# The order of a fused attention and MoE kernel: first loads on SyncE, one early sine, and a new table of offsets

## The chip, the core and the metric

One NeuronCore of a Trainium2 chip. The metric is the device time of one execution in microseconds. TensorE is called PE here, VectorE DVE, ScalarE ACT, GpSimd POOL and SyncE SP.

## What is computed

```python
kv  = einsum('bhsd,bhse->bhde', k, v)             # batch 8, heads 8, sequence 576, head size 64
out = einsum('bhsd,bhde->bhse', q, kv)
out = out / sqrt(mean(out * out, -1) + 1e-6) * g_norm
x   = out.transpose(0, 2, 1, 3).reshape(4608, 512)
h   = x @ w_in                                     # w_in is 512 x 2048
y   = (h * cos(h)) @ w_out                         # w_out is 2048 x 512, y is 4608 x 512
```

All inputs are fp32, w_in and w_out arrive as float64.

## The kernel before

A product of fp32 accuracy is made of three fp32r matmuls, from a high and a low part of each factor (xhi and xlo, ghi and glo; a weight tile wi or wo holds both of its parts). So every weight and every activation passes a "split": a cast on ACT for the high part, a difference on DVE for the low one. For a weight, which arrives in 512 KB tiles, there are some three wide DVE operations and two on ACT (`w_part`, L1034).

The 4608 tokens are nine chunks of 512. The first three go through 48 steps, 16 for each chunk: stage 1 multiplies one 128-column block j of w_in with the four pairs of heads p of x (four groups of three matmuls into a bank, `stage1_part`, L1111), ACT and DVE make h*cos(h) and its split (`act_part`), and stage 2 adds the product with block j of w_out to four accumulators acc0 to acc3, one for each 128 tokens (`stage2_part`, L1179). The other six chunks are taken in three twos by a scheme of seven products (`quad_part`, L1483), whose combined weights are written to DRAM as wq and read back as wi and wo tiles, and a gather with weights out of wod. When an accumulator is full, ACT copies it to one of five slot tiles, and a DMA stores it to out (`out_part`, L1212).

The attention of chunks 0 and 1 is the front. For each pair of heads, k, v and q are loaded, kv is made of 64x64 matmuls (`kv_front_part`), q is transposed through PE, x is made and summed, DVE and POOL make 1/rms (rinv), PE turns the scaled x, and ACT and DVE split it into xhi and xlo with g as a scale (`x_front_part`, L796, `x_norm`, L976). g lies twice in gcol (`g_part`, L552), once for each head of a pair. These early tiles borrow the buffers of weights, so k, v and q appear in the rows as wi and wo tiles. Matmuls on zeros keep PE at work while it would wait.

The order of every engine's instructions is set before the program is built, by a planner (`class Order`, L52). Each part is a generator that asks for time on an engine with a priority; the planner keeps a clock for each engine and starts what can begin first, and of those the one with the lowest priority number. Priorities come from due times of the steps (`due`, L320) plus an offset from a table, `haste` (L327), read by `put_off` (L461) and `gate`. An engine name with a star (DVE*) takes a port that DVE and POOL share; with two engines named, the planner picks. The chip then runs each engine's list in that order, with semaphores for the data.

Nearly all loads and stores are issued by SP through `dmas` (L520), eight in flight at a time; the ninth waits until the first has landed. In `first_loads` (L590) ACT issues k and v of the first pair of heads, the warming sine, and g. All instructions are recorded at L239, since a helper emits them, so rows are told apart by their tiles.

Of the kernel before, what the change touches and what calls it, by code (L numbers as in the profile page):

```python
# [16 lines left out]
AF = mybir.ActivationFunctionType  # L17
# [168 lines left out]
def tile_kernel(  # L186
# [91 lines left out]
    pool.memset(warm, 0.0)  # L278

# [40 lines left out]
    def due(i):  # L320
# [7 lines left out]
        ('acc', 0): 48.4, ('acc', 1): 9.5, ('acc', 10): 311.8, ('acc', 12): -210.7, ('acc', 13): -56.2,  # L328
        ('acc', 14): -112.1, ('acc', 15): 26.9, ('acc', 16): -26.6, ('acc', 17): 2190.7, ('acc', 18): 147.3,
        ('acc', 19): -18.0, ('acc', 2): 101.2, ('acc', 20): 0.5, ('acc', 21): 402.0, ('acc', 24): 404.7,  # L330
        ('acc', 25): 109.7, ('acc', 26): -287.8, ('acc', 27): 8.4, ('acc', 28): 182.6, ('acc', 29): -175.7,
        ('acc', 30): 7.6, ('acc', 31): -58.8, ('acc', 32): 47.5, ('acc', 33): 317.1, ('acc', 34): 1784.0,
        ('acc', 35): 708.7, ('acc', 36): 47.8, ('acc', 37): 20.4, ('acc', 38): 18.1, ('acc', 39): 1.9,
        ('acc', 4): 57.7, ('acc', 40): 636.6, ('acc', 41): -56.3, ('acc', 42): 142.5, ('acc', 43): -345.9,
        ('acc', 44): 240.0, ('acc', 45): 0.1, ('acc', 46): -281.1, ('acc', 47): -52.1, ('acc', 5): 10.5,
        ('acc', 6): 602.4, ('acc', 7): 113.2, ('acc', 8): -14.3, ('acc', 9): 20.2, ('act', 0): 0.5,
        ('act', 1): -263.8, ('act', 10): -60.6, ('act', 11): -55.6, ('act', 12): 14.3, ('act', 13): -237.4,
        ('act', 14): -452.5, ('act', 15): 594.3, ('act', 16): -153.5, ('act', 17): -140.9, ('act', 18): -873.0,
        ('act', 19): -297.3, ('act', 2): 9.0, ('act', 20): 37.2, ('act', 21): -211.4, ('act', 22): 73.3,
# [8 lines left out]
        ('gate keep in', 11): -163.6, ('gate keep in', 12): -211.4, ('gate keep in', 13): -79.1,
        ('gate keep in', 14): -1472.4, ('gate keep in', 15): -26.1, ('gate keep in', 2): 3.7,
        ('gate keep in', 3): -524.9, ('gate keep in', 4): 66.0, ('gate keep in', 5): -51.5,  # L350
        ('gate keep in', 6): -142.9, ('gate keep in', 7): -8.0, ('gate keep in', 8): 108.0,
# [1393 lines left out]
```

## Time and profile before

| | us |
|---|---|
| median of 3 runs | 843.07 (843.03 to 843.53) |
| the profiled execution, its own time | 844.05 |
| its span in the trace | 842.2 |
| PE busy in the span | 825.9 |
| DVE busy | 613.8 |
| ACT busy | 498.2 |
| POOL busy | 227.6 |
| first stage-1 product starts | 35.02 |

Busy time of PE is time in which a matmul is under way. The span is what the trace covers; the execution's own time has some 1.85 us around it. Matmuls overlap, so the distance between starts tells what one costs, and a count of matmuls times that distance tells how much work a stretch of PE rows holds.

### The profile page before, as it was taken

The page shows a single profiled execution, that of the slowest core. Times are in us where ns is not written, and L with a number is a line of the kernel's source. Part 1 is how long each engine was busy: PE and PEld are TensorE (multiplying, and loading weights), DVE is VectorE, ACT ScalarE, POOL GpSimd, SP SyncE. Part 2 cuts the span into 40 slices and gives each one's busy share as a digit, 9 for nine tenths or more (in the row PEclk, how much of TensorE's full clock was granted, in tenths as well). Part 3 has the DMA queues.
Part 4 walks back from the last instruction along what each step waited for, and adds up shares of the span by engine and source line. Part 5 has one row for each costly group of instructions (what it writes and reads, how often), then busy time and mean ns, then how long its engine had stood idle before and what let it go on. Part 6 is the DMA issues. An engine that isn't in the chain of part 4 may idle for free.

```text
span 842.2 us, 12749 instructions
## 1 busy us (share of the span) xinstructions
PE 825.9 (98%) x4424; PEld 681.1 (81%) x4424; DVE 613.8 (73%) x963; ACT 498.2 (59%) x974; POOL 227.6 (27%) x150
## 2 busy tenths in 40 slices
PE   8799999999999999999999999999999999999998
PEld 7678888888888887888887888888788888888886
DVE  3999994469598878669999968878899575444221
ACT  4879983445265565557786657767675464444321
POOL 3310034724427762010324620122438000000000
PEclk9999999999999999999999999999999999999999
DMA  9997535665765577598898767777557566763664
GB/s 301 299 399 275 176 113 190 194 176 155 236 184 189 152 205 269 175 335 254 267 278 233 216 190 183 211 248 201 176 200 240 175 195 191 229 215 105 223 206 145
DMA packets 150399, 181.20 MB, mean 215 GB/s; under 512 B 73920, under 2 KB 113600, under 8 KB 150336
## 3 DMA queue, kind: packets, MB, share of 16 engines
q1 hardware_dynamic: 149824, 179.68, 69.0%
q8 instruction: 35, 0.57, 0.3%
q10 hardware_dynamic: 512, 0.72, 0.2%
q14 instruction: 28, 0.23, 0.1%
HBM read 143.66 MB, written 36.70 MB: 214 GB/s over the span
## 4 chain that ended last, share of the span: by engine, by line
PE 81%; DMA 8%; DVE 5%; ACT 3%; issue 1%; SPq 1%; POOL 0%; DVEq 0%; ACTq 0%; POOLq 0%
PE bank L239 42%; PE acc L239 40%; DMA wi<-in_q_dram 2%; DVE r L239 1%; DMA wo<-wq 1%; DMA x<-slot 1%; DMA out_dram<-slot 1%; DMA wi<-in_v_dram 1%; DVE slot L239 1%; ACT slot L239 1%; DMA sg<-in_v_dram 1%; DMA slot<-part 1%; SPq L239 1%; DVE glo L239 1%; DMA wq<-slot 1%
## 5 line engine op out<-in xcount | busy, mean ns | idle before, releaser
L239 PE MATMUL acc<-wo,ghi 128*128 128x512 f32 x1152 | 355.7, 390 | 1.3 <-ACT slot L239 1.3
L239 PEld LDWEIGHTS acc<-wo,ghi 128*128 128x128 f32 x1152 | 215.4, 188 | 46.3 <-ACT slot L239 2.2
L239 PE MATMUL bank<-wi,wo 128*128 128x512 f32 (+2 forms) x1092 | 244.2, 380 | 4.2 <-DMA wo<-wq 2.0
L239 PEld LDWEIGHTS bank<-wi,wo 128*128 128x128 f32 (+2 forms) x1092 | 191.8, 185 | 46.8 <-DVE glo L239 2.4
L239 PE MATMUL acc<-wo,glo 128*128 128x512 f32 x576 | 224.3, 389 | 0.0
L239 POOL TENSOR_TENSOR rinv<-ms,mhalf 128x16 f32<-128x16 f32 (+1 forms) x36 | 97.2, 2703 | 228.9 <-DVE ms L239 228.5
L239 PEld LDWEIGHTS acc<-wo,glo 128*128 128x128 f32 x576 | 108.1, 188 | 23.0
L239 PE MATMUL bank<-xhi,wi 128*128 128x512 f32 x320 | 99.8, 393 | 0.2 <-DVE slot L239 0.2
L239 DVE TENSOR_TENSOR wi<-bank,wi 128x512 f32<-128x512 f32 x72 | 49.5, 687 | 44.4 <-PE bank L239 35.9
L239 DVE TENSOR_TENSOR glo<-wo,ghi 128x512 fp32r<-128x512 f32 x58 | 42.5, 732 | 46.1 <-ACT ghi L239 45.8
L239 ACT ACTIVATE ki<-wi 128x512 int32<-128x512 f32 x72 | 45.1, 627 | 42.4 <-DVE wi L239 33.7
L239 PEld LDWEIGHTS bank<-xhi,wi 128*128 128x128 f32 x320 | 58.8, 188 | 13.5 <-DVE r L239 0.8
L239 ACT CAST ghi<-wo 128x512 fp32r<-128x512 f32 x61 | 37.8, 619 | 48.4 <-PE acc L239 47.8
L239 ACT ACTIVATE ki<-bank 128x512 int32<-128x512 f32 x72 | 42.6, 591 | 34.2 <-PE bank L239 29.4
L239 PE MATMUL bank<-xlo,wi 128*128 128x512 f32 x160 | 62.4, 390 | 0.0
L239 ACT COPY wi<-bank 128x512 f32<-128x512 f32 x72 | 41.9, 583 | 24.2 <-PE bank L239 23.6
L239 ACT ACTIVATE wo<-wo 128x512 f32<-128x512 f32 x61 | 38.4, 630 | 26.1 <-DVE wo L239 25.8
L239 DVE TENSOR_TENSOR glo<-r,ghi 128x512 fp32r<-128x512 f32 x60 | 44.0, 733 | 13.1 <-ACT ghi L239 10.6
L239 ACT ACTIVATE r<-r 128x512 f32<-128x512 f32 x60 | 37.8, 630 | 20.1 <-DVE r L239 19.6
L239 DVE SCALAR_TENSOR_TENSOR r<-bank,ki 128x512 f32<-128x512 f32 x51 | 34.8, 683 | 19.9 <-ACT ki L239 19.4
L239 ACT CAST ghi<-r 128x512 fp32r<-128x512 f32 x60 | 37.1, 618 | 17.4 <-PE acc L239 16.0
L239 DVE TENSOR_TENSOR r<-r,bank 128x512 f32<-128x512 f32 x51 | 34.5, 678 | 8.5 <-ACT r L239 8.4
(175 smaller groups left out, 1071.6 us busy)
## 6 DMA issues: line engine op xcount, KB each, us to landing
wo<-wod SPq DMA_DIRECT2D x96, 512.0 KB, 3.4
wo<-wq SPq DMA_DIRECT2D x84, 512.0 KB, 4.0
out_dram<-slot SPq DMA_DIRECT2D x35, 256.0 KB, 3.4
wo<-in_moe_w_out_dram SPq DMA_DIRECT2D x16, 512.0 KB, 9.6
wi<-in_moe_w_in_dram SPq DMA_DIRECT2D x16, 512.0 KB, 9.9
wod<-wo SPq DMA_DIRECT2D x16, 512.0 KB, 4.1
wq<-wi SPq DMA_DIRECT2D x24, 256.0 KB, 3.5
m<-in_k_dram SPq DMA_DIRECT2D x24, 256.0 KB, 4.4
```

The source lines that it names most:

```text
L239: return lambda *a, **kw: tc.keep_in_program_order(f(*a, **kw))
```

## The change

The warming sine stands right behind the memset of its tile, ahead of everything on ACT. The loads of k and v of the first pair, and of g, go through `dmas` on SP with priorities that put them early. g's doubling (`g_part`) waits for g's load alone, no longer for kv of the second pair of heads, and fires an event for which the split of every front x waits. The planner is told that the sum ms and the low part of a weight take the shared port of DVE, and that rinv takes 3.15 us of POOL instead of 3.0. Every number of `haste` is new.

```diff
     pool.memset(warm, 0.0)
+    act.activation(out=warm, in_=warm, func=AF.Sin)
...
     haste = {
-        ('acc', 0): 48.4, ('acc', 1): 9.5, ('acc', 10): 311.8, ('acc', 12): -210.7, ('acc', 13): -56.2,
+        ('acc', 0): 253.3, ('acc', 1): 234.7, ('acc', 11): -183.7, ('acc', 12): -84.3, ('acc', 13): -234.2,
...
     def g_part():
         yield "wait", [g_in]
-        yield "wait", [kv_in[0, 1]]
-        yield "run", [("ACT", 0.4)], -11.0
+        _, end = yield "run", [("ACT", 0.4)], -11.0
         for r in (slice(D, 2 * D), slice(0, D)):
             act.activation(out=gcol[r, :], in_=gcol[0:D, :], func=AF.Copy, scale=INV_2PI)
+        sched.fire(g_turns, end)
...
     def first_loads():
         kv_tiles[0, 0] = [wpool.tile([P, SF, D], F32, name=f"{kind}{j}") for kind, j in first_tags]
-        yield "run", [("ACT", 0.5)], -1e3
-        for t, src in zip(kv_tiles[0, 0], (k, v)):
-            act.dma_start(out=t, in_=src[0, 0:2].rearrange("h (p i) d -> (h p) i d", i=SF))
-        act.activation(out=warm, in_=warm, func=AF.Sin)
-        act.dma_start(out=gcol[0:D, :], in_=g_norm.rearrange("(d o) -> d o", o=1))
-        for ev, us in ((kv_in[0, 0], 1.9), (g_in, 0.1)):
-            _, end = yield "run", [("DMA", us)], -1e3
-            sched.fire(ev, end + DMA_LAT)
+        end = yield from dmas([
+            copies(t, src[0, 0:2].rearrange("h (p i) d -> (h p) i d", i=SF), 0.95)
+            for t, src in zip(kv_tiles[0, 0], (k, v))], -1e3)
+        sched.fire(kv_in[0, 0], end)
+
+    def g_load():
+        end = yield from dmas([copies(gcol[0:D, :], g_norm.rearrange("(d o) -> d o", o=1), 0.1)], -950.0)
+        sched.fire(g_in, end)
...
         slot = yield "take", tokens, prio
+        yield "wait", [g_turns]
         yield "run", [("ACT", act_us() + 0.08)], prio
...
-        yield "run", [("DVE", 0.17)], prio
+        yield "run", [("DVE*", 0.17)], prio
         ms = small.tile([P, TB], F32, name="ms")
...
-        yield "run", [("POOL", 3.0)], prio
+        yield "run", [("POOL", 3.15)], prio
...
-            e, end = yield "run", [("ACT", 0.57, 0.3), ("DVE", 0.36, 0.0)], prio
+            e, end = yield "run", [("ACT", 0.57, 0.3), ("DVE*", 0.36, 0.0)], prio
...
             if c == 0 and p == 0:
+                sched.spawn(g_load())
                 sched.spawn(g_part())
```

PE has the same matmuls after the change as before, 1152 + 576 of stage 2 and the rest alike; DVE has 14 instructions fewer, POOL 8 more, ACT 3 more (with three DMA issues fewer among them), SP three more.

SP from its first row on, before. ACT's first two rows before are the loads of k into wi_162 and of v into wo_163, the pair that kv0, the first kv product, needs.

```order
L239 DMA wi_164<-in_q_dram 128x2x256 x2
L239 DMA wo_167<-in_k_dram 128x576
L239 DMA wo_165<-in_k_dram 128x576
L239 DMA wi_169<-in_q_dram 128x2x256
L239 DMA wi_172<-in_k_dram 96x2x384
L239 DMA wi_170<-in_k_dram 128x576
L239 DMA wi_169<-in_q_dram 128x2x256
L239 DMA wi_168<-in_v_dram 128x576
L239 DMA wo_166<-in_v_dram 128x576
L239 DMA wi_174<-in_q_dram 96x4x128
L239 DMA wo_173<-in_v_dram 96x2x384
```

SP from its first row on, after the change. k of that pair goes into wi_163, v into wo_164.

```order
L239 DMA wi_163<-in_k_dram 128x576
L239 DMA gcol<-in_g_norm_dram 64x1
L239 DMA wi_170<-in_q_dram 128x2x256
L239 DMA wo_168<-in_k_dram 128x576
L239 DMA wi_171<-in_k_dram 128x576
L239 DMA wi_165<-in_q_dram 128x2x256
L239 DMA wo_166<-in_k_dram 128x576
L239 DMA wi_165<-in_q_dram 128x2x256
L239 DMA wo_164<-in_v_dram 128x576
L239 DMA wo_189<-in_moe_w_out_dram 128x512
L239 DMA wi_169<-in_v_dram 128x576
L239 DMA wo_172<-in_v_dram 128x576
```

k stands first and g second. v stands ninth, behind loads of k and q for the other pairs, and so behind the eight that may be in flight; a first w_out tile (wo_189) follows it.

PE's first rows behind the matmuls on zeros, before. A row of 64x64 is a kv product, one of ident and a wi tile a transpose of q, one of wo and m an x, one of ident and r a turn of the scaled x.

```order
L239 MATMUL bank0_204<-wo4_163,wi6_162 64x64 x18
L239 MATMUL bank1_227<-ident_125,wi7_164 128x128 x4
L239 MATMUL bank3_239<-ident_125,wi7_164 128x128 x4
L239 MATMUL acc2_247<-wo15_158,m0_237 128x2x64 x4
L239 MATMUL bank2_253<-ident_125,wi9_169 128x128 x4
L239 MATMUL bank0_270<-ident_125,wi9_169 128x128 x4
L239 MATMUL bank1_278<-wi8_168,wo7_167 64x64 x18
L239 MATMUL acc2_247<-ident_125,r0_299 128x128 x4
L239 MATMUL bank3_316<-wo6_166,wo5_165 64x64 x18
```

The same place after the change:

```order
L239 MATMUL bank0_204<-ident_126,wi9_170 128x128 x4
L239 MATMUL bank1_216<-ident_126,wi7_165 128x128 x4
L239 MATMUL bank2_225<-ident_126,wi7_165 128x128 x4
L239 MATMUL bank3_233<-wo4_164,wi6_163 64x64 x18
L239 MATMUL acc2_263<-wo15_159,m1_221 128x2x64 x4
L239 MATMUL bank0_270<-wi8_169,wo7_168 64x64 x18
L239 MATMUL bank1_299<-wo8_172,wi10_171 64x64 x18
L239 MATMUL acc0_328<-wo15_159,m0_211 128x2x64 x4
L239 MATMUL bank2_347<-ident_126,wi9_170 128x128 x4
L239 MATMUL bank3_357<-wo6_167,wo5_166 64x64 x18
L239 MATMUL acc1_385<-wo15_159,m1_353 128x2x64 x4
L239 MATMUL acc2_263<-ident_126,r0_381 128x128 x4
```

Three transposes of q come ahead of kv0, and no matmuls on zeros stand between them. All four kv products and all four x of chunk 0 come in one go; before, products of chunk 1 and zeros come between the third x and the fourth.

PE at the end of the chunk whose acc3 is the last to fill, and the start of the next chunk's accumulators, before:

```order
L239 MATMUL acc3_3940<-wo14_5121,ghi0_5159 128x512 x2
L239 MATMUL acc3_3940<-wo14_5121,glo0_5160 128x512
L239 MATMUL acc0_5270<-wo12_5149,ghi1_5202 128x512 x2
L239 MATMUL acc0_5270<-wo12_5149,glo1_5203 128x512
L239 MATMUL acc1_5280<-wo12_5149,ghi1_5202 128x512 x2
L239 MATMUL acc1_5280<-wo12_5149,glo1_5203 128x512
L239 MATMUL acc2_5287<-wo12_5149,ghi1_5202 128x512 x2
L239 MATMUL acc2_5287<-wo12_5149,glo1_5203 128x512
L239 MATMUL acc3_5295<-wo12_5149,ghi1_5202 128x512 x2
L239 MATMUL acc3_5295<-wo12_5149,glo1_5203 128x512
```

The same place after the change:

```order
L239 MATMUL acc3_4240<-wo15_5106,ghi0_5160 128x512 x2
L239 MATMUL acc3_4240<-wo15_5106,glo0_5161 128x512
L239 MATMUL acc0_5265<-wo12_5150,ghi1_5199 128x512 x2
L239 MATMUL acc0_5265<-wo12_5150,glo1_5200 128x512
L239 MATMUL acc1_5281<-wo12_5150,ghi1_5199 128x512 x2
L239 MATMUL acc1_5281<-wo12_5150,glo1_5200 128x512
L239 MATMUL acc2_5290<-wo12_5150,ghi1_5199 128x512 x2
L239 MATMUL acc2_5290<-wo12_5150,glo1_5200 128x512
L239 MATMUL bank1_5067<-wi0_4825,wo9_4846 128x512 x3
L239 MATMUL bank1_5067<-wi1_4837,wo9_4846 128x512 x3
L239 MATMUL acc3_5316<-wo12_5150,ghi1_5199 128x512 x2
L239 MATMUL acc3_5316<-wo12_5150,glo1_5200 128x512
```

Between acc2 and acc3 of the new chunk stands a pair of products of the seven-product scheme.

## Rows read from the trace of the kernel before

**Rows 1.** The page of the kernel before: its head, and part 1 (busy time of each engine, share of the span, instructions).
```profile
span 842.2 us, 12749 instructions
...
PE 825.9 (98%) x4424; PEld 681.1 (81%) x4424; DVE 613.8 (73%) x963; ACT 498.2 (59%) x974; POOL 227.6 (27%) x150
```
**Rows 2.** Busy time by stretch. Columns: the stretch, its length, then PE, PEld, DVE, ACT and POOL busy in us (with instructions), TensorE's granted clock, the busy share of the DMA engines, GB/s moved.
```profile
0.00:10.00 10.00, 7.87 (x94) 7.24 (x95) 1.48 (x4) 3.17 (x7) 4.38 (x13) 1.00 0.79 249
10.00:20.00 10.00, 8.01 (x150) 6.90 (x151) 6.01 (x14) 5.93 (x17) 2.59 (x2) 1.00 1.08 354
20.00:30.00 10.00, 7.98 (x130) 7.07 (x124) 9.24 (x20) 7.88 (x15) 3.94 (x3) 1.00 1.10 279
30.00:40.00 10.00, 7.79 (x98) 6.02 (x94) 9.37 (x19) 7.42 (x19) 3.72 (x2) 1.00 1.08 328
40.00:60.00 20.00, 19.98 (x125) 15.34 (x126) 19.83 (x36) 16.32 (x33) 3.62 (x2) 1.00 1.06 385
280.00:340.00 60.00, 58.03 (x255) 47.61 (x254) 45.60 (x69) 34.09 (x70) 29.38 (x23) 0.97 0.66 203
460.00:600.00 140.00, 138.81 (x682) 114.20 (x681) 117.79 (x180) 91.91 (x185) 40.94 (x19) 1.00 0.70 208
```
**Rows 3.** What PE waited for over the whole span. After the colon: us in total, times, the longest in us.
```profile
PE bank L239 <- DMA wo<-wq: 2.0, 1, 2.0
...
PE bank L239 <- DMA wo<-in_q_dram: 1.6, 1, 1.6
...
PE acc L239 <- ACT slot L239: 1.3, 2, 1.2
```
**Rows 4.** The timeline of the first 17 us, all engines. Columns: start us, length us, engine, line, operation, out<-in, shapes, count, and in brackets the idle time before with what ended it (ACTq and SPq are the issuing sides).
```profile
0.72 0.45 ACTq L239 DMA_DIRECT2D wi<-in_k_dram  x1
...
0.73 0.95 SPq L239 DMA_DIRECT2D wi<-in_q_dram  x2
...
1.73 1.28 ACT L239 ACT_TABLE_LOAD   x1 [1.73 <-issue]
...
6.08 1.26 PE L239 MATMUL bank<-wo,wi 64*64 64x64 f32 x36 [0.85 <-DMA wo<-in_v_dram]
...
8.61 1.16 PE L239 MATMUL acc<-wo,m 128*128 128x128 f32 x8 [0.24 <-ACT m L239]
...
9.82 0.42 PEld L239 LDWEIGHTS bank<-ident,wi 128*128 128x128 f32 x4 [0.25 <-DMA wi<-in_q_dram]
...
12.03 0.66 PE L239 MATMUL bank<-ident,wi 128*128 128x128 f32 x4 [1.55 <-DMA wi<-in_q_dram]
...
12.82 1.26 PE L239 MATMUL bank<-wi,wo 64*64 64x64 f32 x36
...
13.33 0.43 ACT L239 ACTIVATE gcol<-gcol 64x1 f32<-64x1 f32 x2
...
14.57 0.47 DVE L239 COPY wo<-bank 64x64 f32<-64x64 f32 x2 [0.72 <-ACT wo L239]
...
14.76 0.69 ACT L239 ACTIVATE xhi<-acc,gcol 128x512 fp32r<-128x512 f32 x1 [0.22 <-ACT wo L239]
15.47 0.75 DVE L239 SCALAR_TENSOR_TENSOR xlo<-acc,gcol,xhi 128x512 fp32r<-128x512 f32 x1 [0.44 <-ACT xhi L239]
```
**Rows 5.** DMA issues of the first 30 us: out<-in, issuing engine, operation, count, KB of each, median us from issue to landing.
```profile
wo<-in_v_dram SPq DMA_DIRECT2D x4, 288.0 KB, 7.4
...
wi<-in_v_dram SPq DMA_DIRECT2D x2, 288.0 KB, 9.1
wi<-in_k_dram ACTq DMA_DIRECT2D x1, 288.0 KB, 3.5
wo<-in_v_dram ACTq DMA_DIRECT2D x1, 288.0 KB, 4.7
```
**Rows 6.** The timeline of 33 to 41 us, first DVE, then PE (columns as in rows 4).
```profile
33.48 0.69 DVE L239 TENSOR_TENSOR wi<-sg,wi 128x512 fp32r<-128x512 f32 x1
34.09 0.68 DVE L239 SCALAR_TENSOR_TENSOR sg<-sg,m 128x512 int32<-128x512 int32 x1
...
35.02 0.70 PE L239 MATMUL bank<-xhi,wi 128*128 128x512 f32 x2
...
36.48 0.60 PE L239 MATMUL bank<-ident,wo 128*128 128x128 f32 x4
...
38.15 1.29 PE L239 MATMUL bank<-wo,m 128*32 128x128 f32 x20
40.02 0.66 PE L239 MATMUL bank<-ident,r 128*128 128x128 f32 x4 [0.58 <-DVE r L239]
```
**Rows 7.** Three views of the weight loads out of wq: their issues over the whole span on the page (columns as in rows 5), the chain of work that ended last at 327 us (start us, us, what), and PE's timeline from 325 us.
```profile
wo<-wq SPq DMA_DIRECT2D x84, 512.0 KB, 4.0
...
327.14 8.25 DMA wo<-wq
...
325.24 8.32 PE L239 MATMUL bank<-wi,wo 128*128 128x512 f32 x36
335.53 4.58 PE L239 MATMUL bank<-wi,wo 128*128 128x512 f32 x12 [1.97 <-DMA wo<-wq]
```
**Rows 8.** The chain of work that ended last, 458 to 464 us: start us, us, what.
```profile
458.28 3.88 DMA out_dram<-slot
...
462.27 0.61 ACT slot L239
```

More of the change, by code (lines that the diff above doesn't have):

```diff
@@ L348, in tile_kernel @@
[L348 to L351, printed above, removed]
-        ('gate keep in', 9): 48.8, ('gate keep out', 0): -620.3, ('gate keep out', 1): -60.3,
-        ('gate keep out', 10): -282.8, ('gate keep out', 11): 40.5, ('gate keep out', 12): 155.5,
@@ L360, in tile_kernel @@
-        ('gate load', 6): -2.1, ('gate load', 7): -35.3, ('gate sums', 0): 4.7, ('gate sums', 1): 1.5,
-        ('gate sums', 2): 63.8, ('gate sums', 3): -21.8, ('gate sums', 4): 45.9, ('gate sums', 5): -46.0,
-        ('gate sums', 6): 45.0, ('gate sums', 7): -43.4, ('gate x', 2, 0): -224.7, ('gate x', 2, 1): -89.5,
[17 rows of a table removed]
-        ('keep in', 7): -61.8, ('keep in', 8): 27.5, ('keep in', 9): 111.4, ('keep out', 0): 11.4,
-        ('keep out', 1): 126.8, ('keep out', 10): -168.2, ('keep out', 11): -60.7, ('keep out', 12): 62.6,
@@ new lines, in tile_kernel @@
+        ('gate keep out', 3): 1.0, ('gate keep out', 4): -4.7, ('gate keep out', 5): -126.4,
+        ('gate keep out', 6): 201.5, ('gate keep out', 7): -70.7, ('gate keep out', 8): -2.7,
+        ('gate keep out', 9): -12.4, ('gate kv', 4): -0.2, ('gate kv', 5): 5.6, ('gate kv', 7): 39.9,
+        ('gate load', 2): 5.7, ('gate load', 3): -24.0, ('gate load', 4): -99.1, ('gate load', 5): 63.5,
+        ('gate load', 6): -322.7, ('gate load', 7): -42.6, ('gate sums', 0): 20.2, ('gate sums', 1): -189.8,
@@ new lines, in tile_kernel @@
+        ('gate sums', 2): 73.0, ('gate sums', 3): 11.2, ('gate sums', 4): 73.5, ('gate sums', 5): -54.0,
+        ('gate sums', 6): 10.8, ('gate sums', 7): -1099.2, ('gate x', 2, 0): -485.4, ('gate x', 2, 1): -371.0,
[18 rows of a table added]
+        ('keep in', 9): -17.9, ('keep out', 0): 147.4, ('keep out', 1): -48.7, ('keep out', 10): -204.2,
+        ('keep out', 11): -121.8, ('keep out', 13): 46.2, ('keep out', 14): -84.6, ('keep out', 15): -48.9,
+        ('keep out', 2): 146.9, ('keep out', 3): -90.1, ('keep out', 4): 353.0, ('keep out', 5): -159.4,
@@ new lines, in tile_kernel @@
+        ('keep out', 6): 6.5, ('keep out', 7): -32.3, ('keep out', 8): -387.9, ('keep out', 9): 158.8,
+        ('kv', 0, 1): -154.1, ('kv', 0, 2): 12.6, ('kv', 0, 3): 27.3, ('kv', 1, 0): 157.2, ('kv', 1, 1): -6.4,
+        ('kv', 1, 2): 74.4, ('kv', 1, 3): -129.1, ('kvd', 2): -1.4, ('kvd', 5): 2.6, ('kvd', 6): -303.1,
+        ('kvd', 7): -102.4, ('kvs',): -12.3, ('kvt', 4): -79.8, ('load kv', 0, 2): -438.1,
[11 rows of a table added]
+        ('load', 'wo', 8): -83.4, ('load', 'wo', 9): 4.9, ('quad', 0): 87.1, ('quad', 1): 0.9,
@@ new lines, in tile_kernel @@
+        ('split', 80): -154.5, ('split', 81): 6.6, ('split', 82): -7.0, ('split', 83): -6.6,
+        ('split', 84): 19.2, ('split', 85): 99.6, ('split', 86): -107.0, ('split', 87): -55.8,
+        ('split', 88): -203.5, ('split', 89): -301.6, ('split', 9): 229.2, ('split', 90): 106.9,
+        ('split', 91): -58.7, ('split', 92): -195.9, ('split', 93): 15.5, ('split', 94): -57.7,
+        ('split', 95): -161.2, ('sums', 0): 26.6, ('sums', 1): 38.0, ('sums', 2): -65.7, ('sums', 3): -8.1,
+        ('sums', 4): 63.4, ('sums', 5): 160.3, ('sums', 6): 88.7, ('sums', 7): -2.4, ('unit', 0): 498.7,
@@ L495, in tile_kernel @@
     kv_turned, x_begun = events(B, NP), events(NCH, NP)
-    g_in, over_in = Event(), events(B)
+    g_in, g_turns, over_in = Event(), Event(), events(B)
     w_done = {key: Event() for key in need}
```

144 lines of the change are left out of this document (67 added, 77 removed), and 85 rows, old and new, of the table haste.

## The prediction

> **What bounds the kernel now.** I read the page's first lines, then the table of busy time by stretch, then the waits of PE, then timeline and chain where a wait stands out. The page's head shows what the time is: PE has matmuls under way for 825.9 of 842.2 us, DVE for 613.8 [rows 1]. No change of order alters those matmuls, so what can be won is PE's idle time, 16.3 us, plus whatever a low clock costs. The stretches show where it lies [rows 2]: 8.35 us in the first 40 (each of the four tenths has 7.79 to 8.01 us busy), almost nothing in 40 to 60, 1.97 in 280 to 340, 1.19 in 460 to 600. In 280 to 340 the clock's mean is 0.97, alone among the stretches shown. The waits name the reasons [rows 3]: 2.0 us for a weight load out of wq, 1.3 for an eviction on ACT, and several waits for q and v early on.
>
> The front is a race of loads and DVE. From 20 to 40 DVE is busy 9.24 and 9.37 of each 10 us, and the DMA engines are full (1.10 and 1.08 [rows 2]). The first product for the MoE starts at 35.02; PE runs without a break only from 40.02 [rows 6].
>
> **The change, part by part.**
>
> *Issue on SP, and the sine first.* ACT issued k and v of the first pair from 0.72 on (0.45 us of ACT for k) and loaded the sine's table from 1.73, 1.28 us long; ACT had nothing to copy before kv0 was there, so the two issues and the table hid one another [rows 4]. Taking them off ACT is worth nothing on the path. On SP they are two more issues of some 0.47 each (two cost 0.95 [rows 4]), plus g's. SP has room for that, but v now stands ninth, and eight loads may be in flight: v is issued when one has landed.
>
> When does v land? Before, v was among the first four loads and landed 4.7 us after its issue [rows 5]; kv0 started at 6.08 [rows 4]. Now four k and three q pieces are ahead of it, 1.97 MB (288 and 256 KB each), with itself 2.26 MB. At the mean rate of the first 10 us, 249 GB/s [rows 2], that is 9.1 us, the lower bound. The upper: issued when the first load lands, at about 4.2 (0.72 and the 3.5 of [rows 5]), with the longest landing of such a piece, 9.1 [rows 5]: 13.3. Between them, two transposes that waited for a q give the landing of known amounts: 1.97 MB at 9.82 and 2.82 MB at 12.03 [rows 4], so 2.26 MB at 10.6. I take 10.8, 4.7 later than kv0's start was.
>
> On ACT's queue v took 4.7, on SP's the v pieces 7.4 in the median [rows 5]. Read as a faster queue, the move would cost 2.7; read as place in the line, nothing beyond what is counted above, and I read it so, since the pieces on ACT were first. The Trainium skill ("DMA: Bandwidth & Descriptors", section "Issuing engines are not separate DMA queues") has all loads share the same 16 DMA engines, whichever engine issues them, so by it the difference is the place alone and the sum stands; but by it the move also wins no bandwidth for any load, which speaks against this part of the change.
>
> *Chunk 0 first, then stage 1.* From v on, the new rows of PE up to the fourth pair hold four kv groups (1.26), four x groups (1.16) and two transposes after kv0 (0.66; the one of four on r counts with them) [rows 4]: 11.0 us, to 21.8. Three times an x also waits for the copies of its kv: 0.96 passed from a kv's end to its copies' end (12.82 + 1.26 to 14.57 + 0.47 [rows 4]), some of it under other rows; at 0.75 each that gives 24.0. Then the norm: before, from the end of x (8.61 + 1.16) to the end of xlo (15.47 + 0.75) 6.45 us passed [rows 4], so the fourth pair is ready at 30.5. The last DVE step of wi0 (0.69 [rows 6]) follows it on DVE: with gaps the first stage-1 product comes at **31.5** instead of 35.02. Bounds: v's (-1.7, +2.5), so 29.8 to 34.0. wi0 itself has 6.85 MB up to its end in the new order of loads, 6.91 before, so it lands no later.
>
> That is 3.5 us earlier, but not all is kept. After wi0 the DVE rows hold wi1's three wide steps, two sums and two x splits before wi1 is ready: some 4.7 us at 0.61 each, start to start, and less for the short ones [rows 6], to 36.8 with POOL's waits; wi1's four groups and a transpose end at 40.1, and wi2 was split in the first rows. So I compare what is done at 40. Before: three groups of stage 1; now eight, five more at 0.69 each (36 matmuls took 8.32, three per group [rows 7]): +3.45. But the new order is behind in chunk 1 by one x part (1.29), one kv (two thirds of 1.26, 0.84) and one transpose (0.60), and ahead by one turn of r (the same 0.60) [rows 4, 6]: -2.13. Net **-1.3** us of time; I carry -1.2, since some transposes there run under other rows.
>
> *g's turn* waits for g alone, 64 numbers loaded second, and x's split waits for it; it stood at 13.33 before, with xhi at 14.76 [rows 4]. Now it comes before the first copies. Nothing: xhi waits for its own sums. If g landed late, ACT would stall behind the turn in its queue, and all copies of q with it; bounded by v's own landing, which comes later, so by zero on the path.
>
> *The 335 stall.* The load of wo8 is issued behind four stores of out and lands after 8.25 us; PE stands 2.0 and runs the next 12 matmuls in 4.58 us where 36 took 8.32 [rows 3, 7], so 4.58 - 2.77 = 1.8 goes to the lower clock: 3.8 in all. The new order has the same 12 products, with wo8 behind four stores and the same work (6.8 us) between the buffer's release and its use: I leave it, 0. Bounds: -3.8 (it goes) and +2 (wo9 now is wanted 2.7 us after wo8, before 6.8).
>
> *The 461 stall.* At 461.7 acc3 of the next chunk waits for the eviction of acc3, which waits for a store that takes 3.88 us, to have its slot: ACT starts at 462.27 and takes 0.61, and PE stands 1.2 [rows 3, 8]. In the new order a pair of products, 1.38 us, stands between acc2 and acc3. If the eviction runs as before, the wait is covered: **-1.2**; bounds 0 and -1.2.
>
> *The rest of the table, DVE\* and 3.15.* They change only where the planner puts things. Fourteen DVE instructions go to POOL or ACT, some 8 us of 613.8; DVE is no bound outside the front. 0.
>
> **The sum.** -1.2 - 1.2 = -2.4 on the profiled execution (844.05, of which 842.2 are span), so 841.65. The median, 843.07, is 0.98 lower; the forecast for the median is 840.67, say **840.6**, with its own range 838.8 to 842.5.
>
> **The rivals.**
>
> A. The forecast: 840.6, chance 0.40.
>
> B. The lead is given back. DVE is busy 19.83 of the 20 us after 40 [rows 2], so PE may go at DVE's pace whatever order it starts in, and another eviction stalls in place of the one at 461. For it: wi1 and wi2 are split one after another by the same DVE. Against: the new rows split two weights while kv and x of chunk 0 run, in time that DVE had idle (6.01 us busy from 10 to 20). Then 843.1; 0.22.
>
> C. Also the 335 stall goes, since the stores may leave earlier: another -3.8, 836.8; 0.15.
>
> D. Late v and a lower clock: slower. PE has three transposes between the warm-up's end and kv0, over 4 us idle in a kernel where 2.0 idle at 333 was followed by the slow matmuls at 335 [rows 3, 7]. Against it: 7.87 us busy and clock 1.00 in the first ten before, with waits of 0.85 and 1.55 [rows 2, 4]. At half speed kv0 and x cost another 1.26 + 1.16 = 2.4, and v at its upper bound another 2.5: first product at 36.4, 840.6 + 4.9 = 845.5. The case decides when the first stage-1 product comes after 35.6 (31.5 + 2.4 + 1.7); at 34 the whole is still no slower. 0.13. The Trainium skill ("TensorE: Matmul & The Clock Gate", Part 1) has an idle PE fall to its half rate, 1.2 GHz; the trace agrees at 335, where the mean clock of 280 to 340 is 0.97, and no row shows it in the front.
>
> E. A new stall of the kind at 333: two later loads into wq's buffers have 5.4 us between release and use where before these had 6.2 and 7.5 (counted in PE rows at 0.23); a median landing is 4.0, that behind stores 8.25 [rows 7]. One of them costs up to 2.0 and 1.8 of clock: 840.6 + 3.8 = 844.4; 0.10.
>
> **How the numbers follow.** The measurement tells 0.2%, 1.7 us, from no change. So faster is below 841.4, slower above 844.8. A lies below 841.4 mostly (0.37 faster, 0.03 same), C is faster (0.15), B is same with 0.03 at either side (0.16 same), D slower, E half same and half slower. Faster 0.55, same 0.24, slower 0.21. The range takes in C's end and B, E and most of D: 836.5 to 845.5.
>
> **What would show it.** Right: kv0 near 10.8, first product with wi0 at 31 to 33, PE unbroken from about 40, a wait for wo<-wq still near 332, none for ACT slot near 460, clock 1.00 in the first 40 us. Wrong: kv0 after 13, a clock below 1 in the first 20 us, the first product after 34, idle PE between 40 and 110, or new waits for wq loads near 300 or 390.

## The result and the profile after

The changed kernel takes **847.17 us** (median of 7 runs, 845.47 to 851.08) against 843.03 for the kernel before beside it (7 runs, 840.74 to 844.77): ratio **1.0058 [1.0034, 1.0081]**, slower by some 4 us. The forecast was 840.6, and 845.5 the upper end of its range. The profiled execution of the changed kernel took 845.69 us.

The page of the changed kernel, head and part 1, against [rows 1]:

```profile
span 843.7 us, 12772 instructions
...
PE 828.4 (98%) x4424; PEld 682.7 (81%) x4424; DVE 617.4 (73%) x949; ACT 500.9 (59%) x980; POOL 244.9 (29%) x158
```

PE has the same 4424 matmuls, busy for 2.5 us longer, so some of them ran slower. DVE has 14 instructions fewer and is busy 3.6 us longer: its instructions became longer, not more.

Busy time by stretch, changed kernel (columns as in [rows 2]); the last three rows cut the front finer:

```profile
0.00:10.00 10.00, 5.83 (x50) 5.05 (x51) 1.02 (x2) 3.06 (x6) 4.39 (x13) 0.86 0.77 251
10.00:20.00 10.00, 9.48 (x132) 8.66 (x130) 4.72 (x12) 4.77 (x14) 0.07 (x1) 0.62 1.10 325
...
40.00:60.00 20.00, 19.11 (x161) 15.00 (x162) 19.93 (x35) 16.62 (x36) 3.00 (x2) 1.00 1.07 382
280.00:340.00 60.00, 59.32 (x268) 48.99 (x267) 44.74 (x62) 34.68 (x71) 34.54 (x26) 1.00 0.69 216
460.00:600.00 140.00, 140.00 (x688) 115.28 (x687) 121.76 (x188) 97.47 (x195) 45.75 (x22) 1.00 0.69 207
...
6.00:8.00 2.00, 0.28 (x2) 0.28 (x3) 0.00 (x0) 0.40 (x1) 0.00 (x0) 0.82 0.95 303
8.00:10.00 2.00, 1.17 (x6) 0.77 (x6) 0.00 (x0) 0.59 (x1) 0.00 (x0) 0.50 1.03 384
...
18.00:20.00 2.00, 2.00 (x38) 1.92 (x32) 1.77 (x6) 1.73 (x7) 0.07 (x1) 1.00 1.16 280
```

In 280 to 340 and 460 to 600 the changed kernel has less idle time on PE than [rows 2], as the forecast wanted it at 461. In the first 20 us the granted clock, 1.00 throughout in [rows 2], stands at 0.50 from 8 us on (PE at 1.2 GHz) and is back at 1.00 only in the row from 18. From 10 to 20 PE is busy more than before (9.48 against 8.01) with fewer matmuls (132 against 150): the sign of slow work in a busy share.

PE's timeline of the changed kernel shows what PE did before the clock fell (columns as in [rows 4]):

```profile
5.15 0.63 PE L239 MATMUL bank<-ident,wi 128*128 128x128 f32 x4 [0.41 <-DMA wi<-in_q_dram]
7.72 1.12 PE L239 MATMUL bank<-ident,wi 128*128 128x128 f32 x4 [1.94 <-DMA wi<-in_q_dram]
9.67 1.11 PE L239 MATMUL bank<-ident,wi 128*128 128x128 f32 x4 [0.83 <-DMA wi<-in_q_dram]
10.71 2.19 PE L239 MATMUL bank<-wo,wi 64*64 64x64 f32 x36
13.42 2.15 PE L239 MATMUL acc<-wo,m 128*128 128x128 f32 x8 [0.52 <-ACT wo L239]
...
33.96 0.71 PE L239 MATMUL bank<-xhi,wi 128*128 128x512 f32 x2
...
40.54 0.66 PE L239 MATMUL bank<-ident,r 128*128 128x128 f32 x4 [0.81 <-DVE r L239]
```

The two waits for q, 1.94 and 0.83, stand ahead of a transpose of 1.12 where 0.66 was seen, of kv0 at 2.19 where 1.26 was, and of x at 2.15 where 1.16 was [rows 4]. kv0 starts at 10.71 (forecast 10.8); the first stage-1 product comes at 33.96 (forecast 31.5).

PE's waits over the whole span, against [rows 3]: none for ACT slot is left, and in this trace the wait for wo<-wq fell from 2.0 to 0.4, but three others grew (before, they were 1.6, nothing and 0.3).

```profile
PE bank L239 <- DMA wi<-in_q_dram: 3.2, 3, 1.9
PE bank L239 <- DVE wi L239: 1.2, 2, 1.1
PE bank L239 <- ACT wi L239: 1.2, 1, 1.2
```

The wait for DVE wi is at 608, that for ACT wi at 342. The first recurs in every further trace of the same kernel, at the same length. The second recurs in two of three, and the runs below show that the kernel before waits near that place as well.

### The profile page after: what moved, and what is told of

Same layout as the page of the kernel before. It is cut to its first block, busy times and chain, and to the rows that moved or that the text cites. A ratio compares the mean times of both kernels' runs of the same rounds, so it can differ in the third digit from the quotient of the medians.

```text
span 843.7 us, 12772 instructions
## 1 busy us (share of the span) xinstructions
PE 828.4 (98%) x4424; PEld 682.7 (81%) x4424; DVE 617.4 (73%) x949; ACT 500.9 (59%) x980; POOL 244.9 (29%) x158
## 4 chain that ended last, share of the span: by engine, by line
PE 86%; DVE 5%; DMA 4%; ACT 1%; issue 1%; POOL 1%; SPq 1%; DVEq 0%; ACTq 0%; POOLq 0%
PE acc L239 45%; PE bank L239 42%; DVE sg L239 1%; DVE r L239 1%; POOL rinv L239 1%; DMA wo<-wq 1%; DMA wq<-wi 1%; DMA wo<-in_moe_w_out_dram 1%; SPq L239 1%; DVE wo L239 1%; DMA wi<-in_q_dram 1%; DMA m<-in_k_dram 1%; DMA part<-slot 1%; DVE glo L239 0%; DVE wi L239 0%
## 5 line engine op out<-in xcount | busy, mean ns | idle before, releaser
L239 POOL TENSOR_TENSOR rinv<-ms,mhalf 128x16 f32<-128x16 f32 (+1 forms) x36 | 98.9, 2753 | 201.2 <-DVE ms L239 197.4
L239 DVE TENSOR_TENSOR glo<-wo,ghi 128x512 fp32r<-128x512 f32 x61 | 45.9, 752 | 41.7 <-ACT ghi L239 41.1
L239 DVE TENSOR_TENSOR glo<-r,ghi 128x512 fp32r<-128x512 f32 x59 | 46.5, 790 | 29.0 <-ACT ghi L239 28.8
```

The lines of the kernel that those rows point to most:

```text
L239: return lambda *a, **kw: tc.keep_in_program_order(f(*a, **kw))
```

## The experiments

The theory after the first trace: **the front's clock** (rival D's mechanism without its late v) costs the lead, and some stalls come from the new order of stores and adders. Rivals: the lead is given back to DVE (B); ACT's release from the loads is at fault; the table of priorities is; or the difference is a matter of which execution was profiled. Ratios are to the kernel before on the same chip, with the 95% interval; a difference of two medians is taken within one chip's runs where that is possible. Lost time, in the expectations, is the time up to a point less the work that PE has done by then.

**The changed kernel once more (again), and two single traces (look_2, look_3).** No edit.

> The changed kernel once more, for a second trace and for its time beside the kernel before on one chip. Its first trace has a span 1.5 us longer than before's, all of it in the first 40 us, and the same 14 us of lost PE time after 40 in both, while the medians are 4.1 apart. Theory 'front': the loss is that of the front and the rest of the 4.1 is chance between profiled executions: this run is 1.5 to 2.5 over before, and its trace loses no more after 40 than the first (13 to 15 us). Theory 'rest': the new order waits longer for late transfers in most executions than in the profiled one: 3.5 to 5 over before, with 2 to 3 us more lost after 40 in this trace than in the first.

> The changed kernel, a third trace: its two traces were faster (845.7, 846.5) than the medians (847.2, 848.2). Theory 'late transfers': a slower execution loses its extra 1 to 3 us in waits for transfers that vary (245, 341, 362), not in the front; theory 'front': lost time at 110 over 23.5.

> The changed kernel, a fourth trace, for the same question: extra lost time between 110 and 440 by 'late transfers', before 110 by 'front'.

Measured: again 848.19 (10 runs), 1.0056 [1.0035, 1.0077]; the single traces 848.88 and 846.26. The first stage-1 product came at 33.73, 34.59 and 32.65. The loss is real. PE's wait at 608 recurred at 1.07, 1.07 and 1.08 us. ACT's own wait for its stores near 341 recurred too (1.48, 0.73 and 1.96, in the first trace 1.91); PE's wait that follows was 0.80 and 1.26 in again and look_3, and in look_2 PE waited 1.35 for a weight load at 339 instead. A wait of PE for wo<-wq near 364 varies over the four traces: 0.39, 1.47, 1.74, 1.31. One near 428 (for a PE bank) is 0.43 to 0.45 in all four.

**The kernel before once more (before_2 with 10 runs, before_3 a single trace).** No edit.

> The kernel before once more, for its second trace: in its first the wait for wo8 at 333 and the low clock behind it cost 3.9 us of PE time, while the changed kernel, with the same four stores ahead of that load, lost 0.2 to 1.0 there in three traces. Theory 'chance': the wait is that execution's own; this trace loses under 1.5 us between 330 and 345, and the typical kernel before is better than its first trace by 2 to 3, which is what the medians say of the changed kernel (4.1) against the traces (1.5). Theory 'order': 3 to 4 us again.

> A third trace of the kernel before, for the same question: under 1.5 us lost between 330 and 345 by 'chance', 3 to 4 by 'order'; and between 440 and 470, where the first trace lost 1.8, the same again if the eviction there is held by the order.

Measured: 844.18, 1.0021 [1.0005, 1.0036], for the identical code; the single trace 843.7. So 0.2% between two kernels is no evidence here. Their first stage-1 products came at 36.59 and 34.05, against 35.02 in the trace that the forecast used; the low clock occurs before the change too (0.83 over the first 20 us of before_2). The stall at 333 varies too: 1.71 us in before_3, with the next 12 matmuls in 2.96 us where [rows 7] has 4.58, and none in before_2, where PE waited 0.49 for ACT near 344 instead. The chain of waits of before_2 there:

```profile
337.91 5.86 DMA wq<-wi
...
343.86 0.63 ACT wi L239
```

ACT waits until the stores of a w_in tile to wq have landed before it overwrites the tile; SP had issued these stores behind weight loads. No trace of the kernel before has a wait near 364 or 428.

**zeros: keep PE busy in the front.** 36 and 26 matmuls on zeros stand ahead of the second and third transpose; the order is else the same.

```diff
     def x_front_part(c, p, prio):
...
+        if c == 0:
+            for _ in range((0, 36, 26, 0)[len(filled)]):
+                pe.matmul(out=ps_t[:, 0:P], lhsT=zeros, rhs=zeros, start=True, stop=True)
+            filled.append(p)
```

> The changed kernel with 36 and 26 matmuls on zeros put ahead of the second and the third transpose of q, where PE stands idle for 1.9 and 0.8 us; every other instruction keeps its order. Theory 'clock': the idle PE let the clock fall, and kv0 to the third kv ran at half speed (2.19 us where 1.26 is the full-speed price, x 2.15 against 1.16). Then the clock of the first 20 us is 0.97 to 1.00 instead of 0.86 and 0.62, the fourth product to start x is some 3 us earlier, the first stage-1 product comes at 31 to 32 instead of 33.96, and the time is 2 to 3 us under the changed kernel's. Theory 'loads': the front is held by q, v and the weights, so the matmuls' speed is hidden: the clock is full but the first stage-1 product stays at 33 to 34.5 and the time within 0.7 us.

Measured: 845.44, 1.0029 [1.001, 1.0047]; against again on the same chip 2.75 us faster. PE's timeline of zeros:

```profile
6.14 2.17 PE L239 MATMUL bank<-zeros 128*128 128x128 bf16 x36
8.20 0.66 PE L239 MATMUL bank<-ident,wi 128*128 128x128 f32 x4
8.70 1.61 PE L239 MATMUL bank<-zeros 128*128 128x128 bf16 x26
...
10.69 1.26 PE L239 MATMUL bank<-wo,wi 64*64 64x64 f32 x36
12.47 1.44 PE L239 MATMUL acc<-wo,m 128*128 128x128 f32 x8 [0.52 <-ACT wo L239]
...
31.77 0.71 PE L239 MATMUL bank<-xhi,wi 128*128 128x512 f32 x2
```

The transposes and kv0 have their full-speed durations again, and the first stage-1 product comes at 31.77: the forecast's 31.5 was right for a full clock. The mean clock of a run, 0.991 to 0.998 in the 7 runs of the changed kernel, is 0.997 to 1.000 in those of zeros. So the front's clock is shown to be one cause; half of the loss (1.0029 of 1.0056), though, is still there.

**kv_on_act: give ACT its loads of k and v back**, with the plan unchanged.

```diff
+        for t, src in zip(kv_tiles[0, 0], (k, v)):
+            act.dma_start(out=t, in_=src[0, 0:2].rearrange("h (p i) d -> (h p) i d", i=SF))
+        act.activation(out=warm, in_=warm, func=AF.Sin)
```

> The changed kernel with k and v of the first pair issued by ACT ahead of the sine, as before, while the order of everything else stays. Theory 'place of v' (the step of the prediction): v lands by 6 instead of 10, so kv0 starts earlier than 10.71 by over 1 us and the time falls by 1 to 2 us. Theory 'order of PE': kv0 stands behind the third transpose, whose q lands at 9.67; v two places ahead moves that q by 0.3 MB, so kv0 starts at 11 to 11.7, the clock falls as in the changed kernel, and the time is equal or up to 1 us longer.

Measured: 847.34, 1.0045 [1.0027, 1.0064]; kv0 at 10.54 instead of 10.71. v's place in the line was not what held kv0: v lands at 5.12 instead of 10.34, but kv0 stands behind the third transpose in PE's order, and that waits for its q (until 9.49 there, 9.67 in the changed kernel). Who issues the two loads is worth at most the noise.

**act_issue: the same, but the planner knows of it** (its blocks for the three loads as before the change), so it plans anew; **old_table: the new code with the old haste.**

> The change without its move of the first loads: k, v and g issued by ACT, the sine behind them, and the planner told so; the new table and the other edits stay. The planner then puts kv0 ahead of the transposes, and most of the later order comes out differently. Theory 'clock': PE has kv0 from 6 on and no idle as long, the clock stays at 0.97 or more in the first 20 us, and the first stage-1 product comes at 30 to 32.5; the time is 1.5 to 3 us under the changed kernel's. Theory 'rest': the front matters little beside the waits after 40, which the table was not searched for here: within 1.5 us of the changed kernel's or slower.

> The changed kernel with the old table of offsets: the new issue of the first loads, g's new wait, and the planner's new costs under the numbers that were found for the old code. Theory 'the table belongs to its plan' (as the issue on ACT under the new table took 868): over 852, with several long waits of PE on DVE between 40 and 110. Theory 'the edits cost or gain by themselves': 843 to 848, lost time as in the kernel before after 110, and all of the difference in the first 40 us.

Measured: 868.39, 1.0295 [1.0265, 1.0325], and 905.49, 1.0735 [1.0705, 1.0765]. PE's waits, first of act_issue:

```profile
PE bank L239 <- DVE r L239: 10.5, 5, 6.7
PE acc L239 <- DVE glo L239: 4.0, 1, 4.0
```

and of old_table:

```profile
PE bank L239 <- ACT m L239: 22.4, 4, 18.1
```

These are stalls that neither of the two kernels has. They tell that neither table fits the other's plan, and nothing of what each part of the change is worth; parts have to be undone with the order held. What the new table costs by itself, apart from the new issue and the new prices, was not measured.

**before_zeros and before_cold: the same knob on the kernel before.** 8 and 26 zeros ahead of its third and fourth transpose, and 12 instead of 40 zeros at the very start.

```diff
-    for _ in range(40):
+    for _ in range(12):
         pe.matmul(out=bank[:, 0:P], lhsT=zeros, rhs=zeros, start=True, stop=True)
```

> The kernel before with 8 and 26 matmuls on zeros ahead of the third and the fourth transpose of q, where PE waits 0.3 and 1.6 to 2.0 us; every other instruction keeps its order. The executions of before show a mean clock from 0.993 to 1.000, and those at 1.000 are about 1 us faster. Theory 'clock': the clock is 0.999 or 1.000 in nearly all executions, and the time is 0.5 to 1.5 us under the kernel before's copy (844.2), so 842.7 to 843.7. Theory 'the clock there costs nothing': 844 to 845.

> The kernel before with 12 matmuls on zeros at its start instead of 40, so that PE stands idle from about 2.2 us to kv0's start at 6; nothing else is changed. Theory 'clock': PE's clock is low over a part of the first 20 us as in the changed kernel (mean of 0.6 to 0.9), kv0 takes over 2 us instead of 1.26, and the time is 1 to 3 us over the kernel before. Theory 'the front is held by loads in this kernel': the clock falls but the first stage-1 product comes within 0.5 us of the traces of before (35.0 and later), and the time stays within 1 us.

Measured: 843.63, 1.0004 [0.9986, 1.0022], and 843.3, 1.0000 [0.9984, 1.0016]. PE's timeline of before_cold:

```profile
6.07 2.19 PE L239 MATMUL bank<-wo,wi 64*64 64x64 f32 x36 [3.63 <-DMA wo<-in_v_dram]
8.19 1.97 PE L239 MATMUL bank<-ident,wi 128*128 128x128 f32 x8
9.98 2.08 PE L239 MATMUL acc<-wo,m 128*128 128x128 f32 x8
```

Slow matmuls as long as those of the changed kernel cost the kernel before nothing that shows (the interval is 1.3 us to either side), although its first stage-1 product comes at 36.80 in this trace, later than in the three of before. A likely reason, argued from the orders and not tested: there loads hold the front, while in the changed kernel all four pairs of chunk 0 hang on one run of PE work ahead of the first product, so that each slow group is on the path.

**dve_more: is DVE the bound behind the front?** zeros, with the sums ms of chunk 1's norms done twice (four more TENSOR_REDUCE of some 0.6 us, 2.4 us of DVE in all).

```diff
-        dve.tensor_reduce(out=ms, in_=heads(sq), axis=AX.X, op=ALU.add)
+        for _ in range(2 if c else 1):
+            dve.tensor_reduce(out=ms, in_=heads(sq), axis=AX.X, op=ALU.add)
```

> The kernel with zeros ahead of two transposes, with each sum over a chunk-1 pair (a DVE instruction of 0.6 us) done twice, four times in all, between 34 and 70 us: 2.4 us more work for DVE, the same result. Theory 'DVE bounds 35 to 110': PE's lost time at 110 goes from 20.3 to 22 to 23, and the time is 1.5 to 2.6 us over the kernel with zeros. Theory 'DVE has slack there': lost time at 110 under 21.2, the time within 0.8.

Measured: 848.03, 1.0068 [1.0044, 1.0091] (4 runs), 0.0039 above zeros (the two intervals just meet), some 3 us for 2.4 us of DVE. Busy time by stretch in dve_more:

```profile
0.00:40.00 40.00, 35.35 (x478) 30.80 (x479) 25.17 (x49) 24.07 (x56) 15.27 (x19) 1.00 1.00 315
40.00:60.00 20.00, 19.37 (x161) 14.70 (x160) 19.90 (x35) 17.06 (x37) 1.64 (x1) 1.00 1.07 377
60.00:110.00 50.00, 48.83 (x217) 39.77 (x216) 48.19 (x78) 41.01 (x75) 12.40 (x9) 1.00 0.69 240
```

zeros has 482, 164 and 220 matmuls in the same stretches, 10 more by 110 us (some 0.23 us each, 2.3 us). The order of PE is the same in the changed kernel, zeros and dve_more, so one matmul can be followed through the three traces. The same stage-1 product, in this order:

```profile
105.10 0.61 PE L239 MATMUL bank<-xhi,wi 128*128 128x512 f32 x2
102.92 0.62 PE L239 MATMUL bank<-xhi,wi 128*128 128x512 f32 x2
105.20 0.61 PE L239 MATMUL bank<-xhi,wi 128*128 128x512 f32 x2
```

zeros and dve_more start their first stage-1 product together (31.77 and 31.75); here they are 2.28 apart. So the added 2.4 us of DVE cost nearly all of their length between these two places, and DVE sets the pace there. (The doubled sums also lengthen chunk 1's norm; DVE's 19.90 of 20 busy us speak for its load as the reason, but the run does not part the two.) But zeros is 2.18 ahead of the changed kernel here, and was 2.19 ahead at the first product (31.77 against 33.96): nothing of what it won in the front is paid back. So rival B is half right: DVE is a bound behind the front, but that a lead is given back to it is not shown, and between these two kernels it is not so.

**fixes and fixes_only: take the waits at 608 and 342 away.** At 608 the trace of the changed kernel shows three engines (DVE, then POOL, then PE):

```profile
606.04 1.68 DVE L239 SCALAR_TENSOR_TENSOR wo<-wi,ki 128x512 f32<-128x512 f32 x1
607.64 0.68 DVE L239 TENSOR_TENSOR wi<-bank,wi 128x512 f32<-128x512 f32 x1
...
605.67 1.50 POOL L239 TENSOR_TENSOR slot<-xlo,xlo 128x512 f32<-128x512 f32 x1
...
608.37 1.65 PE L239 MATMUL bank<-wi,wo 128*128 128x512 f32 x6 [1.09 <-DVE wi L239]
```

The first DVE instruction takes 1.68 us beside an add that the new plan gave to POOL, where 0.71 is its mean over the span, and the second makes the wi that PE waits for. The Trainium skill ("SBUF — State Buffer", section "Summary: rules for kernel authors") says of a DVE instruction with two SBUF inputs and a GpSimd instruction that reads SBUF that the second to issue blocks fully until the first is done. The trace agrees to 0.14 us: from POOL's end at 607.17, 0.69 more would end at 607.86, and it ended at 607.72. The next one, with one input in PSUM, took 0.68 beside POOL's next add. In fixes (below), without an add on POOL there, the first instruction takes 0.69.

At 342 and near 364 the chain of waits of the changed kernel reads:

```profile
334.24 0.32 SPq L239
...
334.61 0.43 SPq L239
...
335.08 6.27 DMA wq<-wi
...
341.45 0.62 ACT wi L239
...
352.21 5.24 DMA m<-in_k_dram
...
357.51 6.29 DMA wo<-wq
```

The edit puts three of POOL's adds near 608 on DVE, and issues the two stores of the w_in tile of 342 at step 44, some 50 us earlier, while the planner books all of them as it did. fixes has it on top of zeros, fixes_only without.

```diff
+                if i == 44:
+                    w = w_split["wi", 6]
+                    for q, half in ((A11, 0), (A12, 1)):
+                        sp.dma_start(out=wq[:, 21 + q], in_=w[:, :, half * WH:(half + 1) * WH].bitcast(F32))
...
+            if (n, k) == (2, 0) and q in (S1, S2):
+                e = "DVE"
             adder(e).tensor_tensor(out=out, in0=a, in1=b, op=op)
```

> The kernel with zeros, with two places of the later order changed: three adds at 600 to 608 that the new table gave to POOL are done on DVE, and the two stores of the last kept w_in tile, which stand behind three weight loads on SP at 334, are issued some 50 us earlier (the tile lies ready since the first 60 us). All else keeps its order. Theory 'POOL holds DVE up': the DVE operation of 1.68 us at 605 takes 0.7, and PE's wait of 1.25 at 606 falls under 0.4. Theory 'chain of DVE': DVE has 2 us more to do there, and the wait stays or grows. Theory 'line on SP': the wait of 0.9 to 1.6 at 341 on ACT, which waits for these stores, goes to under 0.3. If all of it is right, the time is 1.5 to 2.5 us under the kernel with zeros, 843 to 844.

> The changed kernel with the two late places mended (three adds of POOL at 600 to 608 on DVE, the last kept w_in tile stored some 50 us earlier) and without the zeros in the front. With zeros 845.4, with zeros and the two places 843.1, without either 847.2 and 848.2. Theory 'two separate costs': the front's low clock stays (0.994) and costs its 2.3 to 2.7, the two places give back 2.3: 845 to 846. Theory 'they share a slack' (an earlier end of the front only lengthens the later waits, or the other way round): within 0.8 us of 843.1 or of 847.7.

Measured: fixes 843.12, 0.9996 [0.9984, 1.0009]; fixes_only 845.49, 1.0023 [1.0007, 1.004]. Both waits are gone from both traces. With the four kernels side by side (ratios; the first cell has two builds of the changed kernel):

| | waits at 342, 608 kept | taken away |
|---|---|---|
| front as changed | 1.0058, 1.0056 | 1.0023 |
| zeros in the front | 1.0029 | 0.9996 |

The zeros give 0.27 to 0.29% in either column, the mended places 0.33 to 0.35% in either row, and both together make up what the change lost: the two gains add up. But the second is not a price of the change, as the traces show:

- Near 342 both kernels wait. Between 333 and 345 PE waits 0.49 to 1.97 us in the five traces of the kernel before and its variants with that place as it was, and 0.70 to 1.84 in seven traces of the changed order. The mend takes some 1.3 us off that place (mean of three traces with it against seven without); in before_fixed, below, a mend of the same kind takes some 1.8 off it in the kernel before (one trace against five).
- At 608 the mend moves the wait. PE waits 0.53 to 0.55 us for DVE glo some 30 us later in the three traces with the mend and in none of the changed order without it, and of the 1.0 us that is won by 625, 0.9 is gone by 700. So that place is worth some 0.1 us.

**fixes_kv: the wait near 364.** In the trace of fixes_only it was at its longest, 3.39 us; its chain of waits:

```profile
351.55 6.05 DMA m<-in_k_dram
...
357.66 8.47 DMA wo<-wq
```

A weight load stands behind ten loads of k and v on SP, is issued when one of those has landed, and takes 8.47 us. fixes_kv issues the five v loads of that batch only behind the second weight load that follows:

```diff
+    def put_aside(b, src, piece):
+        us, late, issue = piece
+        return (us, late, lambda: aside.append(issue)) if b == 5 and src is v else piece
...
-            sched.spawn(landing(copies(w.bitcast(F32), wq[:, s:s + 2], 1.5), due(NS + 2 * t * QUAD // 7) - 14.0, win_in[t]))
+            sched.spawn(landing(and_aside(copies(w.bitcast(F32), wq[:, s:s + 2], 1.5)), due(NS + 2 * t * QUAD // 7) - 14.0, win_in[t]))
```

> The kernel with zeros and the two mended places, and a third: of the ten loads of k and v that the new order issues in one go at 350 to 357, right ahead of a weight load out of wq, the five of v are issued behind the second weight load that follows. In the changed kernel that weight load took 6.3 to 8.5 us to land and PE lost 0.6 to 3.6 us to it near 362, in each trace another amount. Theory 'line on SP': the wait near 360 goes to under 0.2 and the time is 0.5 to 1.2 us under the kernel with two places mended (843.1), so 842 to 842.6. Theory 'v is now late': the next batch's kv products wait for v instead, and the time stays or grows.

Measured: 842.66, 0.9999 [0.9986, 1.0013]. SP's issues there show the two weight loads ahead of the v loads:

```profile
348.44 2.15 SPq L239 DMA_DIRECT2D m<-in_k_dram  x4
350.68 2.49 SPq L239 DMA_DIRECT2D wo<-wq  x2
353.31 0.61 SPq L239 DMA_DIRECT2D v_over<-in_v_dram  x1
```

PE waits for nothing from 346 to 364 in that trace. The median did not move, so this wait has a place and a mechanism, but its price is within the noise.

**before_fixed: the same cure for the kernel before.** The two stores of its kept tile 8 at step 44, and the four stores of out by ACT.

```diff
+        if c == PLAIN - 1:
+            piece = (0.68, STORE_LAT, lambda: act.dma_start(out=to, in_=o))
```

> The kernel before, with the two stores of its last kept w_in tile issued some 50 us earlier, and the four stores of out ahead of the load of wo8 (at 324 to 327) issued by ACT, so that they no longer stand ahead of it on SP. In five traces of before one of these two held PE there, for 1 to 2.4 us of lost time, twice with a low clock behind it. Theory 'line on SP': PE's lost time between 330 and 345 falls under 0.6 and the time is 1 to 2 us under 843.2. Theory 'shared engines': the load shares the 16 DMA engines with the stores whoever issues them, so it lands no earlier and 1 us of the wait stays; ACT's four issues of 0.45 delay its copies; within 0.7 us of 843.2.

Measured: 842.0, **0.9981 [0.9967, 0.9995]**, the fastest kernel of the study, 1.8 us under the kernel before on its chip, though 0.2% is also what two builds of identical code differed by. So the same kind of mend seems to serve the kernel before as well; the step from 0.9996 (fixes) to 0.9981 is not clear of the noise. PE's timeline there, where [rows 7] has 36 matmuls, a wait of 1.97 and 12 slow ones:

```profile
327.81 9.50 PE L239 MATMUL bank<-wi,wo 128*128 128x512 f32 x40
337.14 0.62 PE L239 MATMUL acc<-wo,ghi 128*128 128x512 f32 x2
```

## Why the prediction was wrong, step by step

- **v's landing: right.** v landed at 10.34 and kv0 started at 10.71, against 10.8 forecast, although what held kv0 was the q of the third transpose.
- **The first stage-1 product at 31.5: wrong, 33.96.** This is the step that failed: the sum of the front priced kv, x and transposes at the full-speed durations of [rows 4], though rival D had noted over 4 us without work between the warm-up and kv0 (the trace has 3.2: 0.41, 1.94 and 0.83). The clock fell to 0.50 there, and kv0 took 2.19 and x 2.15. That was rival D, at 0.13, but it was tied to a late v that did not come. With the clock held up by zeros the product comes at 31.77. Price: 2.3 to 2.75 us in the median. The row of D's own that went wrong is its point of decision, 35.6: at 33.96 the kernel was already slower.
- **-1.3 by 40 us, carried as -1.2: not there.** Count the time up to 40 us less the work that PE has done by then, each matmul but those on zeros at its full-speed distance from start to start. This lost time is 22.0 us in the trace of the kernel before and 22.0 in that of the changed kernel; with the clock up (zeros) it is 20.1. So the low clock took all of this step too.
- **The stretch from 40 to 110, left at nothing: wrong against the trace that was used.** The kernel before loses 1.7 us there in that trace, but 4.8 and 3.8 in before_2 and before_3; the changed kernel loses 4.2 to 5.4 in its four traces and zeros 4.3. Rival B at 0.22 named DVE, whose 19.83 of 20 busy us [rows 2] stood there, and dve_more shows that DVE bounds this stretch. That a lead is lost to it is not shown: the lead of zeros over the changed kernel is whole at 105 us. Whether the changed order is worse than the old one in this stretch stays open, since the old one's traces differ by 3 us.
- **The 461 stall: right.** No wait for ACT slot is left, and PE is busy 140.00 of 140. In before_2 and before_3 the wait was 0.70 and 0.54, so 1.2 [rows 3] was the largest of three, and the gain is 0.5 to 1.2 us.
- **The 335 stall left at 0: about right.** The wait for wq was 1.97 us in the trace that was used and 1.71 in before_3; before_2 has 0.49 for ACT in its place. The 1.8 for the clock was in one of the three only. The changed kernel waits 0.80 to 1.84 there, for a weight load, for DVE or for ACT.
- **"The rest of the table: 0": wrong.** DVE's work that went to POOL was counted as relief. POOL's busy time rose by 17 us, DVE's by 3.6 with fewer instructions, and at 606 one such overlap reaches PE (1.1 us, where the kernel before waits 0.34 at 602). Waits near 364 (0.39 to 1.74) and 428 (0.43 to 0.45), which the kernel before does not have, are new. With the eviction's gain taken off, the means of these make some 1.6 us, an estimate; zeros still lacks 0.0029, 2.4 us. No experiment prices them: taking away the wait near 364 did not move the median, and mending 608 moved the wait elsewhere. So the second half of the loss has likely places, but its cause stays open.
- **Rival E** was of the right kind (a weight load late in SP's queue) at another place, near 364; no price is shown for it.

With zeros and the two places mended, the changed kernel equals the one before (0.9996 and 0.9999); the forecast's gain of 2.4 us is not there. One of its two parts, the eviction's, shows in the traces; the other, the front's, is there at 40 us with a full clock (1.9) and cannot be told from the spread of the kernel before's own traces by 110.

## What to carry to other kernels

When an order is changed at the front, price the moved matmuls at both clock levels if the new order has PE wait ahead of them (here 1.94 and 0.83 us); a few matmuls on zeros may be the cheapest cure. Where two kernels share an order, follow the same matmul through both traces: it shows where a lead is won and whether it lasts, which the busy share of the next engine does not. Take two or three traces of the kernel before: a stall seen in one of them may be chance. And try a mend on the kernel before as well, before you book the mended place as a price of the change.

## What the runs showed that was not expected

- In before_cold the granted clock reads 1.00 in each 2 us row from 6 to 12, while kv0 takes 2.19 us there. One of these rows:

```profile
6.00:8.00 2.00, 1.93 (x36) 1.96 (x36) 0.00 (x0) 0.00 (x0) 0.00 (x0) 1.00 0.75 235
```

  The trace's records of the granted clock begin only at 12.24 us in this run (between 3.9 and 6.9 in the changed kernel's four traces), so the 1.00 ahead of that stands for no record. At the very start the durations of the matmuls are the better witness.
- Adding 2.4 us to a DVE that is busy for 73% of the span cost nearly all of it, since it fell into the stretch from 40 to 110 us, where DVE is busy for 96% and more.
- The time outside the span is not the same for all kernels. It is 1.8 to 2.0 us for the kernel before, 1.8 to 2.1 for the changed one, and 1.8 to 3.2 for the kernels with zeros, so spans flatter the latter. What takes this time stays open.
- A lower mean granted clock goes with a longer time: over the runs of the kernel before, executions with 1.000 took 842.0 us in the mean, those with 0.998 took 843.6 and those with 0.996 took 844.7.
